# Attention mask of blocks 1 to 4: added by VectorE as scores leave PSUM, in place of two mask products on TensorE

## The chip, the core and the metric

The kernel runs on one core of one Trainium2 chip. The metric is the time of one execution on the device, in microseconds (us); the number that counts is the median of several runs.

## What is computed

The reference chains three stages. Only the first is touched by the change.

```python
# 1. windowed attention: batch 4, 8 heads, 576 positions, head size 64
scores = scale * np.matmul(q, k.transpose(0, 1, 3, 2))
rel = pos[:, None] - pos[None, :]
mask_plain = (rel >= 0) & (rel < 32)                          # heads 0 to 3
mask_dil = (rel >= 0) & (rel < 128) & (rel % 4 == 0)          # heads 4 to 7
scores = np.where(masks, scores, -1000000000.0)
scores = scores - np.max(scores, axis=-1, keepdims=True)
attn = np.exp(scores)
attn = attn / (np.sum(attn, axis=-1, keepdims=True) + 1e-09)
x = np.matmul(attn, v)                                        # to 2304 tokens x 512
# 2. gated layer: 512 -> 1536 -> 512
x = (sigmoid(x @ w_gate) * (x @ w_val)) @ w_out
# 3. soft mixture of 8 experts with 4 slots each (phi, w1, w2)
```

## The kernel before, in words

The 2304 tokens are cut into five blocks: blocks 0 to 3 are the first 512 positions of each batch entry, block 4 the last 64 positions of all four. A block has four **units**, one for each pair of heads, in the order `HP_ORDER = [0, 2, 1, 3]`. Block 0 is done first by itself. The 16 units of blocks 1 to 4 are called unit 0 to unit 15 here: units 0 to 3 are block 1, 12 to 15 block 4.

One unit goes through these steps:

- `scores`: TensorE fills two PSUM banks, one for each head (`s_ps`, pool `ps_a`). First one product a bank with the identity as weights and the bf16 mask as data (L148, 128x256), which writes 0 or a very negative number; then 32 small products of q and k (L162), which add to it.
- `weighted`: the products of attention weights and v for the unit two before (L222) go into the free columns of the same two banks.
- `softmax`: VectorE takes the row maximum of each bank (L176, two instructions), subtracts it (L178, two, which also bring the scores to SBUF, tile `sm` or, in block 4, the unit's own `qk` tile); ScalarE takes the exponential (L184); VectorE sums (L186), adds 1e-9 (L187), inverts (L188); GpSimd scales (L189).
- `turn_unit`: TensorE transposes the result (L195), ScalarE copies it out (L196).
- `finish_unit`: the weighted values leave PSUM through ScalarE (L237, L250) and VectorE (L238, L251).

These 16 units are spread, by the list `sab`, among the products of the gated layer of blocks 0 and 1 (`l1`, L470). There a **sum** is 12 products of 128x512 into one PSUM bank (pool `ps_l1`, two banks, used in turn); each of the 12 weight strips f has two sums, a = 0 (gate, taken out by ScalarE at L480) and a = 1 (value, taken out by VectorE at L456). The weights are split in two parts for exactness: ScalarE copies the high part (L433), VectorE or GpSimd subtracts it to give the low part (L434), into `whl`, a ring of two. The weights themselves arrive as 64-bit numbers and are converted first (`convert`): ScalarE L379, VectorE L380 and L381, GpSimd L382 (the sum of both halves into `fw`). Converted output weights are transposed by TensorE (L408, into `wt_ps`) and multiplied on (L414, L423).

Each engine runs its own instructions in order. TensorE's order around the units is the order in which the code is written (`at` keeps it there); the other engines' orders come from a scheduler that knows the priorities and what each instruction depends on. All loads and stores named here go through one queue, that of SP, in its order.

## Time and profile before

| | |
|---|---|
| median of 3 runs | 498.02 us (497.69 to 499.08) |
| the profiled execution | 496.94 us, of which the span of instructions is 495.2 us |
| TensorE (PE) busy | 468.6 us, 95% of the span |
| TensorE weight load (PEld) busy | 357.3 us, 72% |
| VectorE (DVE) busy | 311.0 us, 63% |
| ScalarE (ACT) busy | 213.1 us, 43% |
| GpSimd (POOL) busy | 156.8 us, 32% |
| mean granted TensorE clock | 0.992 of full speed |

Times in rows are counted from the first instruction. Matmuls are pipelined, so a row's duration of one product is longer than the step to the next; what a product costs TensorE is read from the starts of its neighbours. An engine's idle time costs nothing unless the engine is the one that sets the end.

### The profile page before, as it was taken

The page shows a single profiled execution, that of the slowest core. Times are in us where ns is not written, and L with a number is a line of the kernel's source. Part 1 is how long each engine was busy: PE and PEld are TensorE (multiplying, and loading weights), DVE is VectorE, ACT ScalarE, POOL GpSimd, SP SyncE. Part 2 cuts the span into 40 slices and gives each one's busy share as a digit, 9 for nine tenths or more (in the row PEclk, how much of TensorE's full clock was granted, in tenths as well). Part 3 has the DMA queues.
Part 4 walks back from the last instruction along what each step waited for, and adds up shares of the span by engine and source line. Part 5 has one row for each costly group of instructions (what it writes and reads, how often), then busy time and mean ns, then how long its engine had stood idle before and what let it go on. Part 6 is the DMA issues. An engine that isn't in the chain of part 4 may idle for free.

```text
span 495.2 us, 12830 instructions
## 1 busy us (share of the span) xinstructions
PE 468.6 (95%) x5488; PEld 357.3 (72%) x5488; DVE 311.0 (63%) x629; ACT 213.1 (43%) x414; POOL 156.8 (32%) x132
## 2 busy tenths in 40 slices
PE   6889999999899998999889999999999999999993
PEld 3558888887788876886557888888887889742552
DVE  3879898758666745436987656655547765541532
ACT  2455645435445534314744554554535343300223
POOL 0244536416445314235154323334212124110100
PEclk9899999999999999999999999999999999999998
DMA  8979978995896079120002201201499886579997
GB/s 301 421 276 361 351 234 306 310 344 195 322 368 253 2 253 394 63 86 1 1 1 86 85 25 61 86 5 80 142 372 422 345 326 259 190 296 367 428 402 239
DMA packets 23785, 112.14 MB, mean 226 GB/s; under 512 B 2352, under 2 KB 7216, under 8 KB 14640
## 3 DMA queue, kind: packets, MB, share of 16 engines
q1 hardware_dynamic: 23408, 111.06, 60.0%
q8 instruction: 43, 0.70, 0.6%
q10 hardware_dynamic: 320, 0.26, 0.2%
q14 instruction: 14, 0.11, 0.1%
HBM read 97.16 MB, written 14.16 MB: 225 GB/s over the span
## 4 chain that ended last, share of the span: by engine, by line
PE 80%; DVE 8%; DMA 4%; ACT 2%; issue 2%; POOL 1%; SPq 1%; DVEq 0%; ACTq 0%
PE l1ps L470 32%; PE pa L592 11%; PE pe L592 6%; PE tp L757 3%; PE s_ps L222 3%; PE h_ps L1045 3%; PE lt_ps L721 3%; PE pd L592 3%; PE s_ps L162 3%; PE so_ps L1104 3%; DMA wo<-fw 2%; PE sp L786 2%; PE tr L195 2%; DMA qk<-qkv 2%; DVE s L556 1%
## 5 line engine op out<-in xcount | busy, mean ns | idle before, releaser
L470 PE MATMUL l1ps<-x_hi,whl 128*128 128x512 f32 x384 | 129.4, 402 | 2.6 <-ACT x_hi L250 2.5
L470 PEld LDWEIGHTS l1ps<-x_hi,whl 128*128 128x128 f32 x384 | 71.7, 188 | 19.0 <-ACT x_hi L250 3.2
L470 PE MATMUL l1ps<-x_lo,whl 128*128 128x512 f32 x192 | 75.6, 394 | 0.0
L382 POOL TENSOR_TENSOR fw<-fw 128x512 int32<-128x512 int32 x36 | 49.0, 1370 | 61.7 <-DVE fw L381 24.7
L470 PEld LDWEIGHTS l1ps<-x_lo,whl 128*128 128x128 f32 x192 | 36.2, 188 | 6.6 <-DVE x_lo L251 0.2
L456 DVE SCALAR_TENSOR_TENSOR g<-g,l1ps 128x512 f32<-128x512 f32 (+1 forms) x36 | 21.4, 594 | 29.3 <-PE l1ps L470 29.0
L470 PE MATMUL l1ps<-x,whl 128*128 128x256 f32 x288 | 37.0, 285 | 0.0
L470 PEld LDWEIGHTS l1ps<-x,whl 128*128 128x128 f32 x288 | 35.4, 192 | 0.4 <-issue 0.2
L480 ACT ACTIVATE g<-l1ps 128x512 f32<-128x512 f32 (+1 forms) x36 | 18.9, 526 | 37.4 <-PE l1ps L470 37.4
L434 POOL TENSOR_TENSOR whl<-w,whl 128x512 fp32r<-128x512 f32 x12 | 15.9, 1326 | 51.2 <-ACT whl L433 39.7
L379 ACT ACTIVATE fw<-st 128x512 f32<-128x512 f32 x36 | 22.8, 675 | 12.4 <-DMA st<-wd 9.2
L757 PE MATMUL tp<-cst,g 128*128 128x128 f32 x216 | 28.0, 275 | 0.0
L757 PEld LDWEIGHTS tp<-cst,g 128*128 128x128 f32 x216 | 24.0, 140 | 5.0 <-issue 3.3
L762 ACT COPY gt<-tp 128x512 f32<-128x512 f32 x27 | 15.6, 584 | 25.0 <-PE tp L757 21.9
L176 DVE TENSOR_REDUCE mx<-s_ps 128x4 f32<-128x256 f32 x40 | 15.2, 413 | 14.3 <-PE s_ps L162 8.4
L380 DVE TENSOR_SCALAR fw<-fw 128x512 uint32<-128x512 uint32 x36 | 22.7, 640 | 1.9 <-ACT fw L379 1.0
L655 DVE TENSOR_TENSOR tm<-pe,tm 128x512 f32<-128x512 f32 x12 | 8.3, 691 | 24.1 <-PE pe L592 24.1
L434 DVE TENSOR_TENSOR whl<-fw,whl 128x512 fp32r<-128x512 f32 x24 | 20.9, 884 | 3.7 <-ACT whl L433 3.2
L381 DVE TENSOR_SCALAR fw<-st 128x512 int32<-128x512 uint32 x36 | 17.8, 528 | 7.7 <-DMA wst<-wg 3.7
L189 POOL TENSOR_TENSOR sm<-sm,su 128x512 f32<-128x512 f32 x12 | 13.6, 1130 | 28.3 <-DVE su L188 26.4
L434 POOL TENSOR_TENSOR whl<-wst,whl 128x512 fp32r<-128x512 f32 x12 | 15.9, 1326 | 19.0 <-ACT whl L433 11.7
L433 ACT CAST whl<-fw 128x512 fp32r<-128x512 f32 x24 | 14.6, 620 | 16.1 <-POOL fw L382 11.7
(455 smaller groups left out, 962.1 us busy)
## 6 DMA issues: line engine op xcount, KB each, us to landing
ew<-w SPq DMA_DIRECT2D x32, 1024.0 KB, 7.8
st<-wd SPq DMA_DIRECT2D x18, 1024.0 KB, 9.1
wst<-wg SPq DMA_DIRECT2D x12, 1024.0 KB, 7.7
v<-qkv SPq DMA_DIRECT2D x20, 512.0 KB, 6.1
wg<-fw SPq DMA_DIRECT2D x12, 512.0 KB, 7.8
w<-wg SPq DMA_DIRECT2D x6, 1024.0 KB, 7.5
qk<-qkv SPq DMA_DIRECT2D x10, 576.0 KB, 5.7
qk<-qkv SPq DMA_DIRECT2D x8, 528.0 KB, 5.5
```

The lines of the kernel that those rows point to most:

```text
L176: nc.vector.tensor_reduce(mx[:, 4 * r : 4 * r + 4], u["s_ps"][r], AX.X, ALU.max)
L379: nc.scalar.activation(top, st[:, c, 1].bitcast(F32), AF.Prelu, scale=2.0**-112, alpha=2.0**32)
L380: nc.vector.tensor_scalar(top.bitcast(U32), top.bitcast(U32), 3, None, ALU.logical_shift_left)
L381: nc.vector.tensor_scalar(low.bitcast(I32), st[:, c, 0], 2.0**-29, None, ALU.mult)
L382: nc.gpsimd.tensor_tensor(low.bitcast(I32), top.bitcast(I32), low.bitcast(I32), ALU.add)
L434: (nc.gpsimd if pool[h] else nc.vector).tensor_tensor(whl[:, 1, h], src[:, h], whl[:, 0, h].bitcast(F32), ALU.subtract)
L456: return nc.vector.scalar_tensor_tensor(g, g, 1.0, val, ALU.add, ALU.mult)
L470: nc.tensor.matmul(pt[:, 0:nt], lhsT=whl[:, w_, a, dc, :], rhs=x_[n][:, dc, :], start=first, stop=(dc == HP_ORDER[-1] and w_ == 1),)
L480: nc.scalar.activation(g, pt[:, 0:nt], AF.Tanh, scale=0.5)
L592: nc.tensor.matmul(pt, lhsT=w[:, w_, P * c : P * c + P], rhs=x_[:, c], start=first and c == 0 and w_ == 0 and x_ is hi, stop=c == 1 and w_ ...
L757: nc.tensor.transpose(tp[:, c], g_sb[self.n, 4 * q + c][:, P * j : P * j + P], ident)
L762: nc.scalar.copy(to, tp)
```

## The change

For units 0 to 15 the two mask products are left out, and the first product into each place of the scores starts the sum afresh (`start=True`). VectorE then does four instructions in place of four: two additions of mask and scores (each 128x256, PSUM and SBUF to SBUF), one maximum over the whole 128x512 tile in SBUF, and one subtraction of 128x512 from SBUF to SBUF. Block 0 (`head` is given) runs the old code.

```diff
-            for r in range(2):
+            for r in range(0 if u["added"] else 2):
                 at(
                     nc.tensor.matmul(
                         u["s_ps"][r].rearrange("p t c -> p (t c)"),
...
-                            start=False,
+                            start=u["added"],
...
-        for r in range(2):
-            nc.vector.tensor_reduce(mx[:, 4 * r : 4 * r + 4], u["s_ps"][r], AX.X, ALU.max)
-        for r in range(2):
-            nc.vector.tensor_tensor(
-                s[:, 4 * r : 4 * r + 4],
-                u["s_ps"][r],
-                mx[:, 4 * r : 4 * r + 4].unsqueeze(2).to_broadcast([P, 4, 64]),
-                ALU.subtract,
-            )
+        if u["added"]:
+            n, hp = u["id"]
+            m = mask[:, 2 if n == 4 else (1 if hp >= 2 else 0)].rearrange("p (t c) -> p t c", t=4)
+            for r in range(2):
+                nc.vector.tensor_tensor(s[:, 4 * r : 4 * r + 4], u["s_ps"][r], m, ALU.add)
+            nc.vector.tensor_reduce(mx, s, AX.X, ALU.max)
+            nc.vector.tensor_tensor(s, s, mx.unsqueeze(2).to_broadcast([P, 8, 64]), ALU.subtract)
+        else:
...
-        us = [{"id": j, "z": z} for z, j in enumerate(jobs)]
+        us = [{"id": j, "z": z, "added": not head} for z, j in enumerate(jobs)]
```

The scheduler orders the engines anew. Three places matter below. From line 192 on the changed kernel's lines are numbered 8 higher: its L442 is L434 of before, L464 is L456, L194 is L186, L196 is L188, L388 and L389 are L380 and L381, L416 is L408, L478 is L470.

VectorE around unit 2, before (the maximum is L176, the subtraction L178; `x_lo` belongs to unit 0, `fw` to the conversion of weights, `g` to a value sum):

```order
L176 TENSOR_REDUCE mx_936<-s_ps0_868 128x4
L380 TENSOR_SCALAR fw_845<-fw_845 128x512
L176 TENSOR_REDUCE mx_936<-s_ps1_869 128x4
L178 TENSOR_TENSOR sm4_172<-s_ps0_868,mx_936 128x256
L178 TENSOR_TENSOR sm4_172<-s_ps1_869,mx_936 128x256
L251 TENSOR_TENSOR x_lo_950<-s_ps0_868,x_hi_949 128x2x128
L456 SCALAR_TENSOR_TENSOR g_612<-g_612,l1ps_956 128x512
L186 TENSOR_REDUCE su_942<-sm4_172 128x8
```

The same place now (L179 adds the mask, L180 is the maximum, L181 the subtraction):

```order
L179 TENSOR_TENSOR sm4_172<-s_ps0_864,msk_75 128x256
L388 TENSOR_SCALAR fw_841<-fw_841 128x512
L179 TENSOR_TENSOR sm4_172<-s_ps1_865,msk_75 128x256
L259 TENSOR_TENSOR x_lo_944<-s_ps0_864,x_hi_943 128x2x128
L180 TENSOR_REDUCE mx_930<-sm4_172 128x8
L464 SCALAR_TENSOR_TENSOR g_612<-g_612,l1ps_950 128x512
L181 TENSOR_TENSOR sm4_172<-sm4_172,mx_930 128x512
L259 TENSOR_TENSOR x_lo_944<-s_ps1_865,x_hi_943 128x2x128
L442 TENSOR_TENSOR whl_1016<-fw_841,whl_1016 128x512
L194 TENSOR_REDUCE su_936<-sm4_172 128x8
```

The subtraction now stands behind the value sum's way out (L464), and the sum of the softmax (L194) behind half a weight split (L442).

VectorE at unit 14 (`su_2783` before, `su_2753` now) and the last conversion of output weights (`fw_2664` before, `fw_2636` now), before:

```order
L187 TENSOR_SCALAR su_2783<-su_2783 128x8
L188 RECIPROCAL su_2783<-su_2783 128x8
L381 TENSOR_SCALAR fw_2664<-st_2502 128x512 x2
L418 COPY pt_2836<-pt_ps_2831 128x256
L380 TENSOR_SCALAR fw_2664<-fw_2664 128x512 x2
```

Now:

```order
L195 TENSOR_SCALAR su_2753<-su_2753 128x8
L389 TENSOR_SCALAR fw_2636<-st_2476 128x512 x2
L196 RECIPROCAL su_2753<-su_2753 128x8
L426 COPY pt_2806<-pt_ps_2801 128x256
L388 TENSOR_SCALAR fw_2636<-fw_2636 128x512 x2
```

The reciprocal of unit 14 has moved from ahead of the conversion's first pair to behind it. GpSimd's order is the same in both kernels here: unit 14's scaling, then the two instructions of this conversion, then two weight splits.

TensorE at the same time, in block 1, strips f = 7 and 8 (`l1ps_2844` and `l1ps_2957` before), before:

```order
L408 MATMUL wt_ps_2838<-cst_76,fw_2664 128x128 x4
L470 MATMUL l1ps_2844<-x_hi_949,whl_2804 128x512 x2
L470 MATMUL l1ps_2844<-x_lo_950,whl_2804 128x512
L470 MATMUL l1ps_2844<-x_hi_949,whl_2804 128x512
L148 LDWEIGHTS msk_75
L148 MATMUL s_ps0_2858<-msk_75 128x256
L148 LDWEIGHTS msk_75
L148 MATMUL s_ps1_2859<-msk_75 128x256
L423 MATMUL wp_ps_2941<-cst_76,pt_2836 128x32 x2
L408 MATMUL wt_ps_2945<-cst_76,fw_2664 128x128 x4
L470 MATMUL l1ps_2957<-x_hi_949,whl_2951 128x512
```

Now:

```order
L478 MATMUL l1ps_2814<-x_hi_943,whl_2774 128x512
L416 MATMUL wt_ps_2808<-cst_76,fw_2636 128x128 x4
L478 MATMUL l1ps_2814<-x_hi_943,whl_2774 128x512
L478 MATMUL l1ps_2814<-x_lo_944,whl_2774 128x512
L478 MATMUL l1ps_2814<-x_hi_943,whl_2774 128x512
L431 MATMUL wp_ps_2909<-cst_76,pt_2806 128x32 x2
L478 MATMUL l1ps_2925<-x_hi_943,whl_2919 128x512
L478 MATMUL l1ps_2925<-x_lo_944,whl_2919 128x512
```

The mask products of unit 15 are gone, one product of the sum stands ahead of the first transposes, and the second four transposes have moved to a place behind unit 15's scores and weighted values. Everywhere earlier TensorE's order is that of before without the mask products. SP's order is unchanged.

## Rows read from the trace of the kernel before

**Rows 1.** Windows: length, then busy us (instructions) of PE, PEld, DVE, ACT, POOL.

```profile
34.00:50.00 16.00, 16.00 (x195) 12.51 (x194) 13.63 (x31) 8.27 (x16) 8.06 (x8) 1.00 0.83 303
50.00:70.00 20.00, 20.00 (x313) 16.16 (x314) 18.37 (x31) 10.94 (x20) 10.04 (x8) 1.00 0.84 295
104.00:175.00 71.00, 69.71 (x1322) 56.45 (x1321) 48.55 (x106) 34.21 (x66) 32.17 (x27) 1.00 0.64 236
```

**Rows 2.** TensorE's waits from 34 to 200 us: total, times, longest.

```profile
PE wt_ps L408 <- POOL fw L382: 1.4, 1, 1.4
PE s_ps L222 <- issue: 1.3, 1, 1.3
```

**Rows 3.** TensorE's timeline at unit 2's scores, then at unit 15's: start, duration.

```profile
51.56 0.39 PE L470 MATMUL l1ps<-x_hi,whl 128*128 128x512 f32 x1
51.79 0.39 PE L148 MATMUL s_ps<-msk 128*128 128x256 bf16 x2
52.11 0.86 PE L162 MATMUL s_ps<-qk 64*32 64x64 f32 x64
...
192.85 0.40 PE L470 MATMUL l1ps<-x_lo,whl 128*128 128x512 f32 x1
193.18 0.86 PE L162 MATMUL s_ps<-qk 64*32 64x64 f32 x64
```

**Rows 4.** VectorE's groups from 34 to 200 us: count, busy us, mean ns.

```profile
L434 DVE TENSOR_TENSOR whl<-fw,whl 128x512 fp32r<-128x512 f32 x20 | 17.6, 898 | 2.5 <-ACT whl L433 2.1
...
L176 DVE TENSOR_REDUCE mx<-s_ps 128x4 f32<-128x256 f32 x32 | 12.0, 413 | 7.2 <-PE s_ps L222 5.9 <-PE s_ps L162 1.3
...
L178 DVE TENSOR_TENSOR sm<-s_ps,mx 128x256 f32<-128x256 f32 x24 | 8.9, 410 | 0.0
L186 DVE TENSOR_REDUCE su<-sm 128x8 f32<-128x512 f32 x12 | 8.2, 683 | 3.7 <-ACT sm L184 3.4
```

**Rows 5.** VectorE's timeline from 35 to 65 us; the last row is GpSimd's.

```profile
35.94 0.76 DVE L176 TENSOR_REDUCE mx<-s_ps 128x4 f32<-128x256 f32 x2 [1.31 <-PE s_ps L162]
...
49.27 0.69 DVE L456 SCALAR_TENSOR_TENSOR g<-g,l1ps 128x512 f32<-128x512 f32 x1 [0.54 <-PE l1ps L470]
...
54.09 0.42 DVE L176 TENSOR_REDUCE mx<-s_ps 128x4 f32<-128x256 f32 x1 [0.46 <-PE s_ps L222]
...
62.05 2.39 DVE L434 TENSOR_TENSOR whl<-fw,whl 128x512 fp32r<-128x512 f32 x2
64.36 0.68 DVE L456 SCALAR_TENSOR_TENSOR g<-g,l1ps 128x512 f32<-128x512 f32 x1
64.96 1.28 DVE L434 TENSOR_TENSOR whl<-fw,whl 128x512 fp32r<-128x512 f32 x2
...
62.21 1.68 POOL L382 TENSOR_TENSOR fw<-fw 128x512 int32<-128x512 int32 x1 [0.36 <-DVE fw L381]
```

**Rows 6.** TensorE's timeline at the end of block 0's strip 5, sum a = 0.

```profile
65.28 0.62 PE L470 MATMUL l1ps<-x_hi,whl 128*128 128x512 f32 x2
```

**Rows 7.** The chain that ended last, 174 to 193 us: start, us, what.

```profile
174.85 0.45 PE tr L195 x4
...
177.06 8.92 DMA wo<-fw
...
186.08 0.76 DVE fw L381 x2
...
187.59 1.38 POOL fw L382
...
189.01 0.67 PE wt_ps L408 x4
...
190.95 1.29 POOL whl L434
...
192.28 0.97 PE l1ps L470 x3
```

**Rows 8.** GpSimd's timeline at unit 14's scaling.

```profile
184.69 1.04 POOL L189 TENSOR_TENSOR qk<-qk,su 128x512 f32<-128x512 f32 x1 [8.73 <-PE l1ps L470]
```

More of the change, by code (lines that the diff above doesn't have):

```diff
@@ L174, in softmax @@
         mx = sm.tile([P, 8], F32, tag="mx", name="mx")
-        for r in range(2):
-            nc.vector.tensor_reduce(mx[:, 4 * r : 4 * r + 4], u["s_ps"][r], AX.X, ALU.max)
-        for r in range(2):
-            nc.vector.tensor_tensor(
-                s[:, 4 * r : 4 * r + 4],
-                u["s_ps"][r],
-                mx[:, 4 * r : 4 * r + 4].unsqueeze(2).to_broadcast([P, 4, 64]),
-                ALU.subtract,
-            )
+        if u["added"]:
[6 more added lines that the diff above has]
+        else:
+            for r in range(2):
+                nc.vector.tensor_reduce(mx[:, 4 * r : 4 * r + 4], u["s_ps"][r], AX.X, ALU.max)
+            for r in range(2):
+                nc.vector.tensor_tensor(
+                    s[:, 4 * r : 4 * r + 4],
+                    u["s_ps"][r],
+                    mx[:, 4 * r : 4 * r + 4].unsqueeze(2).to_broadcast([P, 4, 64]),
+                    ALU.subtract,
+                )
         nc.scalar.activation(s, s, AF.Exp, scale=0.125)
```

## The prediction, made before the changed kernel was run

> **What bounds the kernel now.** I read the busy times stage by stage first, then TensorE's waits, then the timelines of TensorE and VectorE around single units, and last the chain that ended last. All 16 changed units lie between 35 and 194 us. There TensorE is busy nearly all the time: 16.00 of 16.00 us from 34 to 50, 20.00 of 20.00 from 50 to 70, 69.71 of 71.00 from 104 to 175 [rows 1]. Its waits in this stretch are few, and the two long ones are 1.4 us in front of the transposes of converted output weights and a gap of 1.3 us inside a run of small products for which no wait is shown [rows 2]. So TensorE sets the pace of the units, and an instruction less on it is time less, as long as what feeds it keeps up. VectorE is the engine next to the limit, but only early: 18.37 of 20.00 us busy from 50 to 70, against 48.55 of 71.00 later [rows 1]. The reader is to see that the change takes work from the engine that bounds and gives it to the one that is nearly full just there.
>
> After the units nothing is changed. What follows starts when the products of blocks 0 and 1 end, so I let it move with them.
>
> **What is removed: 32 mask products.** Their rows say more than they cost, since products overlap. With the pair, the step from the last product of a sum to the first score is 52.11 - 51.56 = 0.55 us; at unit 15, whose pair stands elsewhere, it is 193.18 - 192.85 = 0.33 us [rows 3]. A pair costs 0.22 us, 16 pairs 3.5 us. The first scores now start the sum afresh; they are the same instructions, and no row tells the two kinds of start apart by time: I take 0, and 0 is both bounds.
>
> Two of the 16 save nothing. From the transposes of unit 12 (174.85) the chain leaves TensorE: they free the tile that the next load in SP's queue waits for, behind that load a store goes out at 177.06 and takes 8.92 us, then VectorE, GpSimd and at 189.01 TensorE's L408, in front of which TensorE has waited; GpSimd's weight split releases it once more at 192.28 [rows 2, 7]. The code puts unit 13's pair ahead of unit 12's transposes, unit 14's between them and 189.01, and unit 15's ahead of 192.28. Without the last two TensorE only waits longer. 14 pairs are left: -3.1 us.
>
> **What is added on VectorE.** The additions take the place of the two maxima. The trace has no addition of a bf16 tile to PSUM; the nearest row is the subtraction L178 of the same size out of PSUM, 410 ns, against 413 ns for the maximum that goes [rows 4]. The other bound is the price of twice the elements, 683 ns; I take 410, since the element count is the same. Maximum and subtraction are now of 128x512 each. In a run, a second instruction of 128x512 adds 1.28 - 0.68 = 0.60 us and one of 128x256 adds 0.76 - 0.41 = 0.35 us [rows 4, 5]. So a unit costs VectorE 2 x 0.60 - 2 x 0.35 = 0.5 us more, and 8 us over 16 units.
>
> The subtraction also changes its kind: it has two operands in SBUF, where L178 had one in PSUM. The weight split L434 is such an instruction: two of them take 1.28 us at 64.96, but 2.39 us at 62.05, while GpSimd works from 62.21 to 63.89 [rows 5]; its mean is 898 ns [rows 4]. So a subtraction that meets GpSimd can cost 1.1 us more, one that doesn't nothing.
>
> The Trainium skill, in "SBUF — State Buffer", section "SBUF: two separate sides", says that VectorE with two SBUF operands and GpSimd take a shared port pair in turn, each for a whole instruction. By that rule the rows at 62 us agree (2.39 for 1.28), and each of the 16 subtractions is exposed for the first time; applied to every early one it gives the slower rival below.
>
> **Where VectorE's delay reaches TensorE.** From 104 us on VectorE idles 22 of 71 us [rows 1], and the unit's way from scores to transposes has microseconds to spare; I cost the added work there at nothing. Early it has a price. The tightest place is the way out of the value sum of block 0's strip 4: L456 starts at 64.36 and ends at 65.04 [rows 5], and the sum that takes its PSUM bank starts with the second product of the pair at 65.28, one step of 0.23 later, at 65.51 [rows 3, 6]. That is 0.47 us to spare, while three pairs saved by then make TensorE want the bank 0.66 us sooner. TensorE is thus held by VectorE's lateness plus 0.2 us.
>
> How late is VectorE there? Units 0, 1 and 2 give it 1.5 us more work, one meeting with GpSimd 1.1: 2.6 us. Its idle time from 34 to 70 us is 2.4 + 1.6 = 4.0 us [rows 1], of which 1.3 lies ahead of unit 0 [rows 5]. If all the remaining 2.7 us can be used, it is not late. If only the waits for TensorE can, 0.54 at 49.27 and 0.46 at 54.09 [rows 5], it is 1.6 us late: the other waits are for ScalarE's and GpSimd's part of the weight conversion, which moves with VectorE, and in the new order the exponential of unit 0 stands behind a sum's way out on ScalarE and unit 2's subtraction behind another on VectorE. Both ends are open; I take the middle, 0.9 us late, so TensorE loses 1.1 us (0.2 to 1.8, up to 5 in the rival below). Behind the late L456 stand the next two weight splits, whose sums start some microseconds after, so I charge nothing further.
>
> **What the new order moves at the end.** Unit 14's reciprocal now stands behind the first pair of the last conversion, which cannot start before the store has landed, at 186.08, and runs to 186.84 [rows 7]. GpSimd scales unit 14 after that reciprocal and, in its unchanged order, ahead of L382. Before, the scaling ran from 184.69 for 1.04 us and was long done when L382 started at 187.59 [rows 7, 8]. Now it starts near 187.2 and ends at 188.2 or, if it meets VectorE's next pair, 188.9: L382 starts 0.6 to 1.3 us later, and so do the transposes at 189.01 and the split at 190.95 that TensorE waits for. I take 1.0. If the reciprocal's result came before the store it would be 0. Four transposes that ran ahead of 192.28 now come after it (at most 0.67 us [rows 7]), and one product of 0.23 us ahead: 0.2 more, between 0 and 0.4.
>
> **The sum** is made against the profiled execution, 496.94 us: -3.1 + 1.1 + 1.2 = -0.8 us, 496.1 us. The median of the runs shown is 498.02, 1.1 us above that execution, so the same step gives 497.2 us. About 0.3%, 1.5 us, is what a measurement of this kernel can tell from no change.
>
> **The rivals.**
>
> *The saving comes through.* VectorE uses all its idle time (0.2 us lost), and the last conversion is not delayed: -3.1 + 0.2 = -2.9 us, 495.1 us. For it: TensorE's rows show no wait for VectorE at all now [rows 2], and the new order brings strip 5's first weight split (L442, in the rows of the order) ahead of the softmax sum. Against it: 0.47 us to spare at 65 us, and the reciprocal's new place.
>
> *The port decides: slower.* All three early subtractions meet GpSimd: VectorE is 1.6 + 2 x 1.1 = 3.8 us late at 65 us, or 4.8 if none of the idle time is used; TensorE loses 4.0 to 5.0 us, and the sum is -3.1 + 5.0 + 1.2 = +3.1 us at most, 501.1 us. It counts as slower from a lateness of 3.2 us (-3.1 + 3.4 + 1.2 = 1.5). The place is the same value sum of strip 4. For it: GpSimd is busy half of the time from 34 to 70 us [rows 1], so one meeting in two is likely. Against it: a meeting delays only what is behind it, and the weight splits that met GpSimd before need not meet it again.
>
> *The gap without a wait.* The 1.3 us inside the small products [rows 2] belongs to no engine. With 64 matmuls and weight loads fewer ahead of it, it may vanish (495.9) or a second one may come (498.5), and then the change itself tells little.
>
> **How the numbers follow.** My forecast 0.52, the saving 0.28, the port 0.14, the gap 0.06. The first spans -2.9 (0.2 and 0 lost) to +0.4 us (1.8 and 1.7): 495.1 to 498.4. The range for 8 in 10 goes into the rivals on both sides: 494.8 to 499.6. Faster by over 0.3% (below 496.5): the saving, a twentieth from the first: 0.33. Slower (above 499.5): the port and a little of the gap, 0.15. Within: 0.52.
>
> **What would show it.** The step from the last product of a sum to the first score is 0.33 us, not 0.55; no L148 behind block 0. VectorE has 32 additions near 410 ns, 16 maxima near 685 ns, and 16 subtractions of 680 ns or, where GpSimd runs, up to 1.8 us. TensorE waits 0.3 to 2 us in block 0's strips 4 and 5, with VectorE as releaser. GpSimd's scaling of unit 14 follows the store's landing, and TensorE's wait for L382's successor L390 grows from 1.4 to about 2.6 us. I am wrong if TensorE shows no such waits (the saving), or if its waits for VectorE add up to more than 3.4 us (the port), or if a wait appears that no row of before hints at.

## The result and the profile after

The changed kernel takes 503.93 us (median of 4 runs, 502.77 to 507.68); the kernel before, run beside it on the same chip, 498.55 us (4 runs, 497.69 to 499.74). The ratio is 1.0132, with a 95% interval of 1.0099 to 1.0164: slower by 5.4 us in the medians, where no change was forecast. Medians here and below are of all executions, while ratios and their intervals leave out those over 1.5% above the fastest of their kernel. The profiled execution has a span of 500.9 us (before 495.2) and a mean granted clock of 0.985 (before 0.992); the slowest of the four executions, 507.68 us, has the lowest mean clock, 0.973.

First the windows of the changed kernel; they answer to [rows 1], and the last three have no row there. The columns are start:end, length, busy us (instructions) of PE, PEld, DVE, ACT, POOL, the granted clock, the DMA share and GB/s.

```profile
34.00:50.00 16.00, 16.00 (x192) 12.64 (x192) 14.32 (x29) 8.10 (x15) 6.28 (x6) 1.00 0.84 309
50.00:70.00 20.00, 19.33 (x303) 15.45 (x304) 17.99 (x33) 10.34 (x19) 10.82 (x9) 1.00 0.81 295
104.00:175.00 71.00, 69.49 (x1318) 56.13 (x1316) 55.00 (x108) 35.28 (x68) 33.92 (x26) 1.00 0.65 238
...
190.00:194.00 4.00, 3.47 (x15) 2.70 (x16) 2.07 (x3) 2.66 (x5) 3.26 (x4) 0.76 1.03 418
194.00:198.00 4.00, 3.61 (x120) 2.71 (x120) 1.79 (x2) 0.00 (x0) 1.24 (x1) 0.81 0.86 316
198.00:202.00 4.00, 3.25 (x22) 2.82 (x22) 2.48 (x6) 1.02 (x3) 0.00 (x0) 0.62 0.56 232
```

Up to 175 us little is lost: VectorE does 6.45 us more from 104 to 175, and TensorE is as busy as before. Between 190 and 202 us the granted clock is below 1.00, which it never was there before. TensorE's waits from 34 to 200 us, answering to [rows 2] (total us, times, longest):

```profile
PE wt_ps L416 <- POOL fw L390: 3.2, 1, 3.2
PE s_ps L230 <- issue: 2.4, 3, 1.1
PE l1ps L478 <- DVE g L464: 1.1, 2, 0.7
PE l1ps L478 <- ACT x_hi L258: 0.8, 1, 0.8
PE s_ps L230 <- ACT pt_ring L204: 0.3, 1, 0.3
```

The wait in front of the transposes grew from 1.4 to 3.2 us, and in place of one gap of 1.3 us for which no wait is named ("issue") there are three, 2.4 us together. Where the time went is read from the start of the same product in both traces:

| first product of | before, us | after, us | later by |
|---|---|---|---|
| block 0, strip 0, a = 1 | 29.30 | 29.37 | 0.1 |
| block 0, strip 5, a = 0 | 62.79 | 62.13 | -0.7 |
| block 1, strip 0, a = 0 | 112.04 | 112.47 | 0.4 |
| block 1, strip 4, a = 1 | 155.31 | 154.39 | -0.9 |
| block 1, strip 7, a = 1 | 185.53 | 184.86 | -0.7 |
| block 1, strip 9, a = 0 | 201.38 | 206.72 | 5.3 |
| end of the span | 495.2 | 500.9 | 5.7 |

So the changed kernel is 0.7 us ahead at 185 us, and loses 6.0 us in the next 22 us. TensorE's timeline of the changed kernel there (start, duration; in brackets the idle time before and what ended it):

```profile
190.35 0.66 PE L416 MATMUL wt_ps<-cst,fw 128*128 128x128 f32 x4 [3.16 <-POOL fw L390]
191.08 0.40 PE L478 MATMUL l1ps<-x_lo,whl 128*128 128x512 f32 x1
...
192.26 0.80 PE L478 MATMUL l1ps<-x_hi,whl 128*128 128x512 f32 x1 [0.18 <-ACT whl L441]
192.85 0.63 PE L478 MATMUL l1ps<-x_lo,whl 128*128 128x512 f32 x1
193.28 1.56 PE L478 MATMUL l1ps<-x_hi,whl 128*128 128x512 f32 x3
...
195.84 0.86 PE L162 MATMUL s_ps<-qk 64*32 64x64 f32 x64
196.63 0.98 PE L230 MATMUL s_ps<-pt_ring,v 64*64 64x16 f32 x51
198.75 0.49 PE L230 MATMUL s_ps<-pt_ring,v 64*64 64x16 f32 x13 [1.14 <-issue]
199.17 1.11 PE L416 MATMUL wt_ps<-cst,fw 128*128 128x128 f32 x4
```

A product of 128x512 takes 0.63 us where it took 0.40: that is the granted clock at its lower level, 1.2 GHz for 2.4. The 8 products from 192.26 to 195.84 take 3.58 us, at a step of 0.23 they would take 1.84: 1.7 us lost. The transposes and five products from 199.17 to 202.22 lose about 1.5 us in the same way. The sum: 1.8 us of a longer wait, 3.2 us of a slower clock, 1.1 us for the gap of 198.75, less 0.2 us for a pair of mask products: 5.9 of the 6.0 us. (The wait of 0.18 us for ScalarE has one of 0.15 us for GpSimd in its place before.) The prediction has 1.0 of them.

The chain that ended last, through the wait (it answers to [rows 7, 8]):

```profile
175.98 10.42 DMA wo<-fw
...
186.50 0.76 DVE fw L389 x2
187.26 0.12 DVE su L196
...
187.61 1.28 POOL qk L197
188.90 1.41 POOL fw L390
...
190.35 0.67 PE wt_ps L416 x4
```

The store left 1.08 us earlier than before and landed 0.4 us later (10.42 us for 8.92); the DMA share was 1.00 from 186 to 190 us. Behind it come the conversion's pair, the reciprocal that now stands there, GpSimd's scaling (1.28 us) and only then the sum for the transposes, L390, at 188.90, 1.3 us later than before. This is the step that the prediction named.

### The profile page after: what moved, and what is told of

The parts are those of the page before. It is cut to its first block, busy times and chain, and to the rows that moved or that the text cites. A ratio compares the mean times of both kernels' runs of the same rounds, so it can differ in the third digit from the quotient of the medians.

```text
span 500.9 us, 12758 instructions
## 1 busy us (share of the span) xinstructions
PE 467.9 (93%) x5451; PEld 357.5 (71%) x5456; DVE 322.8 (64%) x629; ACT 213.9 (43%) x414; POOL 157.6 (31%) x132
## 4 chain that ended last, share of the span: by engine, by line
PE 61%; DVE 10%; DMA 7%; ACT 2%; issue 2%; POOL 2%; SPq 0%; DVEq 0%; POOLq 0%; ACTq 0%
PE l1ps L478 20%; PE pa L600 11%; PE pe L600 6%; PE tp L765 3%; PE lt_ps L729 3%; PE pd L600 3%; PE so_ps L1112 2%; DMA ew<-w 2%; PE s_ps L230 2%; DMA wo<-fw 2%; PE sp L794 2%; DMA st<-wd 2%; PE s_ps L162 1%; PE wt_ps L416 1%; PE h_ps L1053 1%
## 5 line engine op out<-in xcount | busy, mean ns | idle before, releaser
L478 PE MATMUL l1ps<-x_hi,whl 128*128 128x512 f32 x384 | 132.0, 408 | 3.8 <-ACT x_hi L258 2.5
L478 PEld LDWEIGHTS l1ps<-x_hi,whl 128*128 128x128 f32 x384 | 73.0, 191 | 21.3 <-ACT x_hi L258 3.2
L478 PE MATMUL l1ps<-x_lo,whl 128*128 128x512 f32 x192 | 76.7, 400 | 0.0
L390 POOL TENSOR_TENSOR fw<-fw 128x512 int32<-128x512 int32 x36 | 48.7, 1359 | 63.5 <-DVE fw L389 27.5
L478 PEld LDWEIGHTS l1ps<-x_lo,whl 128*128 128x128 f32 x192 | 36.8, 191 | 7.0 <-issue 0.4
L464 DVE SCALAR_TENSOR_TENSOR g<-g,l1ps 128x512 f32<-128x512 f32 (+1 forms) x36 | 21.3, 591 | 26.7 <-PE l1ps L478 26.3
L478 PE MATMUL l1ps<-x,whl 128*128 128x256 f32 x288 | 37.0, 285 | 0.0
L478 PEld LDWEIGHTS l1ps<-x,whl 128*128 128x128 f32 x288 | 35.4, 192 | 0.4 <-ACT whl L441 0.2
L442 POOL TENSOR_TENSOR whl<-w,whl 128x512 fp32r<-128x512 f32 x12 | 15.9, 1326 | 51.2 <-ACT whl L441 39.7
L442 DVE TENSOR_TENSOR whl<-fw,whl 128x512 fp32r<-128x512 f32 x24 | 21.4, 902 | 5.5 <-ACT whl L441 4.8
L442 POOL TENSOR_TENSOR whl<-wst,whl 128x512 fp32r<-128x512 f32 x12 | 15.8, 1321 | 28.1 <-ACT whl L441 20.4
L388 DVE TENSOR_SCALAR fw<-fw 128x512 uint32<-128x512 uint32 x36 | 22.1, 630 | 0.5 <-ACT fw L387 0.3
L389 DVE TENSOR_SCALAR fw<-st 128x512 int32<-128x512 uint32 x36 | 19.7, 576 | 4.1 <-DMA st<-wd 2.0
L162 PEld LDWEIGHTS s_ps<-qk 64*32 64x32 f32 x1280 | 14.3, 107 | 9.5 <-issue 7.6
L162 PE MATMUL s_ps<-qk 64*32 64x64 f32 x1280 | 17.7, 228 | 3.3 <-issue 2.0
```

Of the source, the lines that this page charges most:

```text
L162: nc.tensor.matmul(u["s_ps"][r][32 * i : 32 * i + 32, t, :], lhsT=q[64 * r : 64 * r + 64, 128 * t + 32 * i : 128 * t + 32 * i + 32], rhs=k ...
L388: nc.vector.tensor_scalar(top.bitcast(U32), top.bitcast(U32), 3, None, ALU.logical_shift_left)
L389: nc.vector.tensor_scalar(low.bitcast(I32), st[:, c, 0], 2.0**-29, None, ALU.mult)
L390: nc.gpsimd.tensor_tensor(low.bitcast(I32), top.bitcast(I32), low.bitcast(I32), ALU.add)
L442: (nc.gpsimd if pool[h] else nc.vector).tensor_tensor(whl[:, 1, h], src[:, h], whl[:, 0, h].bitcast(F32), ALU.subtract)
L464: return nc.vector.scalar_tensor_tensor(g, g, 1.0, val, ALU.add, ALU.mult)
```

## The experiments

Four theories. **A**: the reciprocal of unit 14, behind the pair that waits for the store, makes GpSimd late; TensorE waits, and its clock falls behind the wait. **B**: VectorE's added work, or its meetings with GpSimd, cost the time. **C**: the gap at 198 us is what lets the clock fall. **D**, formed after the first four runs: TensorE pauses where a piece of its own program lands late, and which instructions that hits depends on how many rows stand ahead of them. The change takes 64 rows (32 weight loads, 32 products) out of TensorE's list.

All were timed in five rounds beside the kernel before on the same chip. Medians in us, ratios to that kernel before; in brackets the 95% interval.

| label | median | ratio |
|---|---|---|
| recip_first | 502.02 | 1.0116 (1.0078 to 1.0153) |
| recip_late | 499.12 | 1.0031 (1.0015 to 1.0048) |
| block1_only | 499.22 | 1.0034 (1.0015 to 1.0054) |
| late_blocks | 503.05 | 1.0095 (1.0063 to 1.0127) |
| first_and_rows_back | 502.37 | 1.0065 (1.0034 to 1.0097) |
| before_rows_fewer | 504.18 | 1.0134 (1.0102 to 1.0166) |
| after_rows_back | 504.10 | 1.0134 (1.0104 to 1.0163) |
| wait_filled | 501.30 | 1.0075 (1.0045 to 1.0106) |
| before_plus_64 | 499.33 | 1.0023 (0.9988 to 1.0059) |
| before_plus_128 | 501.06 | 1.0045 (1.0018 to 1.0072) |
| first_minus_64 | 499.70 | 1.0026 (0.9998 to 1.0053) |
| first_plus_128 | 501.69 | 1.0065 (1.0037 to 1.0092) |
| before_rows_192 | 506.61 | 1.0175 (1.0146 to 1.0203) |
| first_rows_64 | 499.19 | 1.0025 (0.9992 to 1.0057) |
| first_rows_128 | 501.74 | 1.0077 (1.0049 to 1.0105) |
| first_rows_192 | 501.87 | 1.0082 (1.0053 to 1.0112) |
| first_rows_64_filled | 502.07 | 1.0071 (1.0045 to 1.0098) |
| before_filled | 498.68 | 1.0001 (0.9976 to 1.0026) |

**The reciprocal's place.** recip_first is the changed kernel with an edge of order (`behind(x, y)` keeps x behind y on their engine, and waits for nothing), so that VectorE's reciprocal of unit 14 stands ahead of the last conversion's L389; recip_late is the kernel before with the opposite edge. No other row moves in either.

```diff
-            nc.vector.tensor_scalar(low.bitcast(I32), st[:, c, 0], 2.0**-29, None, ALU.mult)
+            low_ = nc.vector.tensor_scalar(low.bitcast(I32), st[:, c, 0], 2.0**-29, None, ALU.mult)
+            pinned_at[i, h] = low_
...
-        nc.vector.reciprocal(su, su)
+        recip = nc.vector.reciprocal(su, su)
+        if u["z"] == 14:
+            for h in range(2):
+                behind(pinned_at[len(turn) - 1, h], recip)   # recip_late: behind(recip, pinned_at[...])
```

> The changed kernel with one edge more: unit 14's reciprocal stands ahead of the last conversion's first pair on VectorE, as before the change; every other row of every engine stands as in the changed kernel. Theory A (the reciprocal that waits for the store makes GpSimd late, TensorE waits 3.2 us for L390's result, and its granted clock falls behind that wait): the wait is back at about 1.4 us, the granted clock stays at 1.0 from 175 to 205 us, and the kernel takes 497 to 498 us, some 6 us less than the changed one and a ratio of 0.997 to 1.000 to the kernel before. Theory B (VectorE's added work or its meetings with GpSimd cost the time, whatever the order): 502 us or more. Theory C (the gap of 1.1 us at 198 us, for which no wait is shown, is what lets the clock fall): the wait's 1.8 us alone come back, 502 us, and the clock still falls.

> The kernel before, mask products and all, with the reciprocal of unit 14 moved behind the last conversion's first pair on VectorE; no other row moves. Theory A: TensorE's wait in front of L408's transposes grows from 1.4 to about 3 us, the granted clock falls behind it, and the kernel takes 4 to 6 us more than before, 502 to 504.5 us, without any added work on VectorE. Theory B: no change, 499 us at most. The prediction's own term for it: 1.0 us more.

The wait moves the way theory A says, to 1.67 us in recip_first (1.4 expected) and to 2.35 us in recip_late (3 expected), as in these two rows of their TensorE timelines.

```profile
189.56 0.66 PE L428 MATMUL wt_ps<-cst,fw 128*128 128x128 f32 x4 [1.67 <-POOL fw L402]
```

```profile
190.32 0.66 PE L420 MATMUL wt_ps<-cst,fw 128*128 128x128 f32 x4 [2.35 <-POOL fw L394]
```

The time doesn't. The reciprocal's place is worth 1.05 us in recip_late (499.12 against 498.07), which is the prediction's term and a quarter of the least that theory A asked for; and putting it back leaves recip_first 4 us slower than the kernel before. Theory A holds for the wait and falls as the whole cause of the loss. The clock fell behind recip_first's wait of 1.67 us and not behind recip_late's 2.35 us. The 502.02 us of recip_first is what theories B and C had named. Theory C falls by the place: in the changed kernel the first slow products start at 192.26, ahead of the gap. Whether the gap had a part in the second fall, at 199 us, is not shown.

**Which blocks.** block1_only and late_blocks (the latter with recip_first's edge) change one condition:

```diff
-        us = [{"id": j, "z": z, "added": not head} for z, j in enumerate(jobs)]
+        us = [{"id": j, "z": z, "added": not head and j[0] == 1} ...   # late_blocks: j[0] > 1
```

> The mask is added by VectorE for block 1 alone (units 0 to 3); blocks 2 to 4 keep their products, and the last conversion has the order of before. Theory A with the prediction's middle term: four pairs save 0.9 us, TensorE loses 1.1 to 1.5 us to VectorE between 60 and 100 us, so +0.2 to +0.6 us, a ratio of 1.000 to 1.002. Theory B: 2 us or more slower. If block 1's price was a matter of one place only and is made good later: -0.9 us.

> The mask is added by VectorE for blocks 2 to 4 alone (units 4 to 15), with unit 14's reciprocal ahead of the last conversion's first pair. Theory A: ten pairs of 0.22 us come through and nothing is lost, -2.2 us, a ratio of 0.995 to 0.997, with no wait of TensorE for VectorE and the granted clock at 1.0 to 200 us; the place of the gap without a wait can add or take 1.2 us. Theory B: no better than the kernel before.

block1_only is 1.15 us slower, more than theory A's 0.6 and less than theory B's 2. From block 0's second sum to block 1's first it loses 0.5 us net, where four pairs saved and the prediction's 1.1 us make 0.2; most of the rest lies at the wait, 1.9 us long, and behind it, where the granted clock fell (0.77 from 188 to 192 us). late_blocks, which has none of the early work, is among the slowest: 1.0095. Theory A's saving of 2.2 us failed there, and theory B's words, no better than before, came true. But its trace shows no wait of TensorE for VectorE from 34 to 206 us; TensorE waited 4.2 us for nothing that the profile names (2.4 us of it at 199 us), and 1.9 us in front of the transposes. That speaks against theory B and for a cause in the gaps and the wait.

**The number of rows, changed in the warm-up.** first_and_rows_back is recip_first with 64 rows put back ahead of the first load's landing, after_rows_back the changed kernel with the same, before_rows_fewer the kernel before with 64 rows fewer.

```diff
-WARM = 8
-SMALL = 70
+WARM = 5       # before_rows_fewer, first_minus_64: 11 and 35
+SMALL = 105    # before_plus_128, first_plus_128: 3 and 139
```

> The kernel of recip_first with 64 rows more in TensorE's list, 32 products of 32 columns with their weight loads, all in the warm-up ahead of the first load's landing: so each row from unit 15 on stands at the number that it had before the change. Theory D (the gap without a wait, 0.9 to 2.4 us at 198 us in every kernel with the mask added in blocks 2 to 4, is TensorE waiting for the next piece of its own program, and comes there because 64 rows fewer stand ahead): no gap at 198 us, the packets of instructions land near 187, 197.5 and 205 us as before the change, no second fall of the clock behind it, and about 499 us, 3 us less than recip_first. Theory A (the long wait for L390's result alone) and theory B (VectorE): no change, 502 us, and the gap stays.

> The kernel before with 64 rows fewer in TensorE's list, taken from the warm-up (the order of a few rows on VectorE in block 0 changes too): the rows behind the units stand at the numbers of the changed kernel, and no mask is added on VectorE. Theory D: a gap of 0.9 to 2.4 us near 198 us, in some executions with a fall of the clock behind it, 1 to 4 us more than before, a ratio of 1.002 to 1.008. Theories A and B: no change.

> The changed kernel with the 64 rows back in the warm-up; the reciprocal stays behind the conversion. Theory D with the reciprocal's term: the gap at 198 us goes, the wait of 3 us and the fall of the clock behind it stay, about 501 us, 3 us less than the changed kernel and 1 to 2 us more than first_and_rows_back. Theories A and B: no change from the changed kernel's 503.9.

before_rows_fewer shows that such a loss needs neither theory A nor theory B: with its mask products in place and no work moved to VectorE it is 1.34% slower, as much as the changed kernel. The largest part of its loss stands in one place, TensorE's timeline of before_rows_fewer:

```profile
137.73 0.41 PE L222 MATMUL s_ps<-pt_ring,v 64*64 64x32 f32 x8 [2.30 <-issue]
138.07 1.11 PE L408 MATMUL wt_ps<-cst,fw 128*128 128x128 f32 x4
138.84 0.77 PE L470 MATMUL l1ps<-x_hi,whl 128*128 128x512 f32 x1
```

a pause of 2.30 us inside a unit's small products, and behind it the slower clock (0.77 us for a product), which took 1.5 us. (The rest, in the profiled execution: 1.5 us at the start, 1.7 us behind another fall of the clock at 445 us.) Theory D expected this pause near 198 us, so the place was missed. In first_and_rows_back and after_rows_back the gap at 198 us is gone, as expected, but one came at 87.6 us in both (2.49 and 1.39 us), in the first with a fall of the clock behind it; neither gained the 3 us. after_rows_back waited 4.5 us in front of the transposes, with a fall behind it. The two differ in the reciprocal's place alone, and their ratios are 1.0065 (1.0034 to 1.0097) and 1.0134 (1.0104 to 1.0163): at this count of rows its place costs 0.7% by the ratios and 1.7 us in the medians, more than recip_late's 1.05 us, so theory A has a part in the loss.

> The kernel before with 64 rows more in TensorE's warm-up, nothing else (two rows of VectorE in block 0 swap). Theory D, as the runs so far have left it (TensorE pauses where a piece of its own program lands late inside a run of small products; which run that is depends on the number of rows ahead of it, and a pause of over 1 us can let the granted clock fall behind it): the time moves by up to 6 us either way, 494 to 504 us, with a gap without a wait at another place than 126.56 us. If the count of rows doesn't matter (theories A and B): 498 us, as before.

> The kernel before with 128 rows more in TensorE's warm-up. Theory D: another time than before_plus_64 and the kernel before, 494 to 504 us, the gap at another place again. Theories A and B: 498 us.

> recip_first (all 16 units' masks on VectorE, the reciprocal ahead of the conversion) with 64 rows fewer in the warm-up. Theory D: the time follows the place of the gap and not the work on VectorE; over the four counts of rows (0, +64, +128, -64) this kernel's times lie among those of the kernel before at its four, within 1 us on their means. Theory B (VectorE's added work): 502 us at every count, 3 to 4 us above the kernel before at the same one.

> recip_first with 128 rows more in the warm-up. Theory D: as for first_minus_64, a time between 494 and 504 us that goes with the place of the gap; with no gap of over 0.5 us from 100 to 205 us it is 496 to 498 us. Theory B: 502 us.

before_plus_64 has no gap over 0.3 us without a named wait from 60 to 206 us, where theory D had one at another place; before_plus_128 has one of 1.66 us at 146.85. With these, each kernel has four counts of rows. The kernel before: 498.07, 499.33, 501.06 and 504.18 us (0, +64, +128, -64), a mean of 500.7. recip_first: 502.02, 502.37, 501.69 and 499.70 us, a mean of 501.4. The kernel before is ahead by 3 to 4 us at two counts, the two are within 1 us at the third, and recip_first is ahead by 4.5 us at the fourth; the means differ by 0.8 us. That is theory D's expectation and not theory B's. What spoils the comparison is the warm-up: with more or fewer of its products the first sum began 0.6 to 3.8 us later than in the kernel before.

**The number of rows, changed inside block 0.** Here the rows are small products behind block 0's value steps (`small(n)` issues n products of 32 columns, each with its weight load), and every other row of every engine keeps its place.

```diff
             if head:
                 keep_warm(WP)
+                small(12)      # 4, 8 or 12: 64, 128 or 192 rows
```

> The kernel before with 192 rows more in TensorE's list (96 products of 32 columns with their weight loads, 12 behind each value step of block 0); every other row of every engine keeps its place. The start costs 1 us at most. Theory D (the count of rows sets where TensorE's pause falls): a pause at another place than 126.56 us, and 499.5 to 504 us, as before_rows_fewer had it, whose rows stand at the same place within a piece of 256. Theory B (VectorE): 498 to 499 us.

> recip_first with 64 rows more, in the same manner (4 small products behind each value step). Theory D: the pause at 198 us goes and one comes elsewhere, at 87 us by the runs with the rows in the warm-up, 500 to 503 us. Theory B: 502 us, pause or no pause.

> recip_first with 128 rows more (8 small products behind each step). Theory D: no pause of over 0.9 us from 60 to 205 us, the end 0.5 us or more ahead of the kernel before once the start's cost is taken off, 496.5 to 499 us. Theory B: 502 us.

> recip_first with 192 rows more (12 small products behind each step). Theory D: as first_rows_128, no pause of over 0.9 us from 60 to 205 us, 496.5 to 499 us, against before_rows_192's 499.5 to 504 at the same count. Theory B: 502 us.

The start costs more than expected: 4 to 7 us at 128 and 192 rows, where 1 us at most was named. The added products themselves are not what costs: TensorE's timeline of before_rows_192 has three pauses there, and 12 products take 0.25 us.

```profile
11.56 0.38 PE L110 MATMUL idle<-pm 128*128 128x512 bf16 x1 [2.90 <-issue]
11.87 0.25 PE L115 MATMUL idle<-pm 128*32 128x32 bf16 x12
...
17.48 0.20 PE L115 MATMUL idle<-pm 128*32 128x32 bf16 x5 [0.82 <-issue]
...
23.60 0.85 PE L165 MATMUL s_ps<-qk 64*32 64x64 f32 x36 [2.98 <-issue]
```

The kernel before has two such pauses at its start, 0.59 and 0.71 us. To leave the start out, I also read the time from the first product of block 0's second sum to the end of the span, in the profiled executions:

| kernel | that product at, us | to the end, us |
|---|---|---|
| before | 29.30 | 465.9 |
| after | 29.37 | 471.5 |
| before_rows_fewer | 30.82 | 471.7 |
| before_rows_192 | 33.44 | 471.1 |
| first_rows_128 | 33.90 | 468.3 |
| first_rows_192 | 36.17 | 464.9 |
| first_rows_64 | 30.13 | 464.7 |

At the same count of 192 rows the kernel with the mask on VectorE is 4.7 us faster than the one without (501.87 against 506.61); at the original count it is 4 us slower. The timeline of before_rows_192 has a pause at nearly the same instructions as before_rows_fewer, whose rows stand at the same place within a piece of 256:

```profile
136.70 1.02 PE L225 MATMUL s_ps<-pt_ring,v 64*64 64x32 f32 x56
139.88 0.44 PE L225 MATMUL s_ps<-pt_ring,v 64*64 64x32 f32 x8 [2.16 <-issue]
...
141.02 0.78 PE L474 MATMUL l1ps<-x_hi,whl 128*128 128x512 f32 x1
141.59 0.63 PE L474 MATMUL l1ps<-x_lo,whl 128*128 128x512 f32 x1
```

and its windows show the clock behind it:

```profile
126.00:138.00 12.00, 11.72 (x287) 9.26 (x285) 8.13 (x17) 4.85 (x10) 6.84 (x6) 1.00 0.99 373
...
140.00:142.00 2.00, 2.00 (x14) 1.76 (x15) 1.63 (x5) 0.60 (x2) 2.00 (x2) 0.50 0.60 141
142.00:146.00 4.00, 4.00 (x11) 3.11 (x10) 0.98 (x3) 0.79 (x2) 0.07 (x1) 0.50 0.99 335
```

Theory D's figures were missed: before_rows_192 came out above its 499.5 to 504 us, first_rows_64 (499.19) below its 500 to 503 and without a pause at 87 us, first_rows_128 and first_rows_192 above their 496.5 to 499. The start ate the gain of the last two, and in first_rows_128 the clock also fell behind a wait of 2.27 us and again at 444 us. What holds is that the count of rows matters: first_rows_64 differs from recip_first in 64 rows alone, and the ratios are 1.0025 (0.9992 to 1.0057) and 1.0116 (1.0078 to 1.0153). (Their medians lie 1.9 and 4.0 us above the kernel before that ran beside them.) The work on VectorE is the same in both, so it is not what makes the difference. Without the start, first_rows_64 and first_rows_192 are 1.0 to 1.2 us ahead of the kernel before: what the mask on VectorE is worth where no long pause and no fall of the clock meet it. This is from one execution each.

**What the pause waits for.** The traces also hold the packets of the queue that carries instructions. Its row in the DMA view of before_rows_192 from 137.4 to 138.5 us, and of the changed kernel from 196.2 to 197.35 us:

```profile
q8 instruction: 1, 0.02, 5.3%
```

```profile
q8 instruction: 1, 0.02, 5.6%
```

One packet of 16 KB lies in each, and none between it and the pause's end (139.88 and 198.75 us). In the 20 traces of this case there are 23 pauses of over 0.6 us from 60 to 206 us that end 1.2 to 1.6 us behind the end of such a packet, 19 of them inside a run of a unit's small products; all the long pauses without a named wait are among them. The data queue fills the DMA engines there (share 0.99 from 126 to 138 us above).

A count settles more. Number TensorE's rows, weight loads and products together, from 0 in the order of their starts. All 23 pauses end at a row whose number is 191 to 194 above a multiple of 256, and so do the 8 shorter ones there, of 0.3 to 0.6 us without a named wait: 4034 = 15 x 256 + 194 for the kernel before at 126.56 us, 6335 = 24 x 256 + 191 for the changed kernel at 198.75. The three pauses at the start of before_rows_192 end at rows 449, 705 and 961, each 193 above such a multiple. And in the 20 whole traces, with 840 packets in all, row 256 n + 196 never started sooner than 1.0 us behind the end of the n-th packet. So each packet holds about 256 rows of TensorE's own program, and the pauses stand where the next piece has not come yet. No row of the profile names this wait; the count leaves little room for another reading. It also says what 64 rows do: they choose which instructions stand at these places.

In the Trainium skill, "Runtime: NRT & Kernel Launch", section "Instruction fetch mechanics", an engine's program arrives in blocks of 16 KiB, that is 256 instructions, and crossing from one to the next is called mostly hidden. The size agrees (43 packets, 0.70 MB, for 10,973 rows of TensorE in the changed kernel), and so does "mostly": of some 350 crossings from 60 to 206 us in the 20 traces 23 show, but as pauses of 0.7 to 2.5 us each.

**The wait filled.** Four products of 128x512 go into the bank that the transposes then overwrite, ahead of them.

```diff
             wt_ps = ps_a.tile([P, ND, P], F32, tag="a", name="wt_ps")
+            for y in range(4 if f == 10 and c == 0 else 0):
+                nc.tensor.matmul(wt_ps.rearrange("p k x -> p (k x)"), lhsT=msk[:, M_ID:M_COLS], rhs=msk[:, 0:512], ...)
```

> first_and_rows_back with four products of 128x512 on TensorE (0.9 us, into the bank that the transposes then overwrite) inside the wait in front of L390's transposes; the rows in the warm-up are fewer by as many. If what TensorE did in the wait decides whether the granted clock falls behind it: the clock at 1.0 from 190 to 200 us in nearly every execution, 1 to 1.7 us less than first_and_rows_back, near 497.5 us. If the clock falls for another reason: no change or 0.3 us more.

> first_rows_64 with four products of 128x512 on TensorE (0.9 us, into the bank that the transposes overwrite) in the wait ahead of L390's transposes; some products behind the wait change places. If the clock's fall behind the wait makes the spread: most executions at 495.5 to 498.5 us, a median of 497, 2 us below first_rows_64's, and hardly one above 501. If the spread comes from elsewhere (the start, the pauses): no change, 499 us.

> The kernel before with the same four products in the same wait. Its wait was 1.4 us and mostly without a fall of the clock behind it: 0 to 0.7 us less than before, a ratio of 0.998 to 1.000. If filling the wait only makes TensorE later: 0.5 us more.

In all three profiles the idle rest of the wait is under 0.9 us and the clock stays at 1.00 behind it; in the 17 profiles with the wait unfilled it fell within some microseconds of it in 8. But the time is not bought: wait_filled is no faster than first_and_rows_back (1.0075 against 1.0065), before_filled is the same as before, and first_rows_64_filled is 2.9 us slower than first_rows_64. In that trace a pause of 1.02 us stands at 86.6 us, VectorE makes TensorE wait 0.5 us at 204.7 us, where products had changed places, and the clock falls at 441 us. The spread between executions of first_rows_64 (496.35 to 505.83 us) is therefore not explained by this wait alone, and stays open. No version beat the kernel before beyond its interval.

## Why the prediction was wrong

The forecast was 497.2 us with no measurable change; measured were 503.93. The step that failed is the sum, -3.1 + 1.1 + 1.2. Behind the last conversion it charges a longer wait with its length alone: 1.0 us for the reciprocal, and of two pairs less it says that "TensorE only waits longer". And it prices all products at the step of 0.23 us, which is that of the full clock. The granted clock behind such a wait is no term of it: it was put at nothing, without a reason. The gap without a wait was kept out of the sum as well. In the profiled execution the stretch from 185 to 207 us lost 6.0 us in their place: 3.2 us to the lower clock, 1.8 us to the wait, 1.1 us to the gap, less 0.2 us for a pair of mask products. The sentence "What follows starts when the products of blocks 0 and 1 end, so I let it move with them" held: 5.3 us late at 207 us, 5.7 at the end.

The sum also counts a removed product as time and not as two rows of the program. The kernel before owes its 498 us in part to where its pauses lie: one of 1.3 us [rows 2], no fall of the clock behind it. Taking 64 rows out without moving any mask costs 1.3% (before_rows_fewer), and 64 rows more in block 0 bring recip_first from 1.0116 to 1.0025 (first_rows_64). What stays open is why the clock falls behind one wait or pause and not behind another of the same length; so the split of the 6.0 us holds for the one profiled execution.

- **The rival that named it was mis-sized.** "The gap without a wait" saw that 64 rows fewer could move or double the gap, at 1.3 us either way and a chance of 0.06. The gaps measured run from nothing to 2.5 us. Behind the four longest, 2.2 to 2.5 us, the clock fell each time (in before_rows_fewer this took 1.5 us more); behind one of 2.05 us it did not.
- **14 pairs, -3.1 us:** right where it can be seen. The step from a sum to the scores is 51.47 - 51.15 = 0.32 us (below), 0.33 forecast; after three pairs TensorE was 0.67 us ahead. But only 0.7 us of the saving was left at 185 us, where the store's landing ended it: the store left 1.08 us earlier and landed 0.4 us later. So what was saved ahead of that wait only made the wait longer. The prediction applied this to two pairs; it held for what was left of all.
- **VectorE's prices:** additions 415 ns for 410, maxima 676 for about 685, subtractions 681 or 781 for 680, in the groups of the changed kernel below. Of the 16 subtractions 13 took 0.68 to 0.69 us, three 0.82, 1.06 and 1.32 us: 1.2 us more for all 16. These three began while GpSimd's sum L390 ran, and each ended 0.54 to 0.55 us behind that sum's end; a fourth, which began 0.16 us ahead of GpSimd's, took 0.68 us. By the rule of the Trainium skill in "SBUF — State Buffer", section "SBUF: two separate sides", whichever of the two starts first holds the shared ports for its whole instruction, and the other waits. These four rows agree. Of the three early subtractions one met GpSimd, as charged, but at 0.14 us and not 1.1.

```profile
L181 DVE TENSOR_TENSOR sm<-sm,mx 128x512 f32<-128x512 f32 x12 | 9.4, 781 | 0.1
L179 DVE TENSOR_TENSOR sm<-s_ps,msk 128x256 f32<-128x256 f32 x24 | 9.1, 415 | 3.4 <-PE s_ps L230 2.3 <-PE s_ps L162 1.1
...
L180 DVE TENSOR_REDUCE mx<-sm 128x8 f32<-128x512 f32 x12 | 8.1, 676 | 0.1
...
L181 DVE TENSOR_TENSOR qk<-qk,mx 128x512 f32<-128x512 f32 x3 | 2.0, 681 | 0.0
```

- **Block 1's +1.1 us:** right in kind and place. TensorE's timeline of the changed kernel, which answers to [rows 3, 6], and VectorE's way out of strip 4's value sum:

```profile
51.15 0.39 PE L478 MATMUL l1ps<-x_hi,whl 128*128 128x512 f32 x1
51.47 0.86 PE L162 MATMUL s_ps<-qk 64*32 64x64 f32 x64
...
64.62 0.39 PE L478 MATMUL l1ps<-x_hi,whl 128*128 128x512 f32 x1
65.68 0.50 PE L478 MATMUL l1ps<-x_hi,whl 128*128 128x512 f32 x1 [0.67 <-DVE g L464]
...
79.87 0.50 PE L478 MATMUL l1ps<-x_hi,whl 128*128 128x512 f32 x1 [0.43 <-DVE g L464]
```

```profile
64.95 0.67 DVE L464 SCALAR_TENSOR_TENSOR g<-g,l1ps 128x512 f32<-128x512 f32 x1
```

  VectorE is 0.6 us late there (64.95 for 64.36 [rows 5]; 0.9 forecast), and TensorE starts its next product at 65.68 and not a step of 0.23 us behind 64.62: 0.8 us lost. Two more such holds, 0.6 us at 79.87 and 0.3 us near 94, were not charged. So from block 0's second sum to block 1's first the net is +0.4 us, where the seven pairs saved by then and 1.1 us lost would have made -0.4. TensorE's waits for VectorE add up to 1.1 us in all, far from the 3.4 of the rival in which the port decides: it is refuted although the time came out on its side.
- **The reciprocal, +1.0 us:** right. GpSimd's scaling stands in the chain as forecast, and recip_late measures 1.05 us. The wait became 3.2 us and not 2.6 us, since TensorE also came earlier. What the term lacks is the clock behind the wait: 1.7 us in the profiled execution, not in each.

## What to carry to other kernels

When an edit adds or removes many short instructions, time both versions at several counts of padding rows before believing either: here the kernel before moved by 1.3% with 64 rows fewer, several times what the edit itself was worth. To see whether a gap without a named wait belongs to the program's pieces, count the rows ahead of it, as above. Read a gap without a named wait as a price that moves with every edit ahead of it, and look at the granted clock behind each long wait. And follow a saving to the next wait that DMA ends: here most of what was left of it was waited out there.

## What the runs showed of the hardware

- TensorE paused 0.7 to 2.5 us without a named wait 23 times, 19 of them inside runs of small products, each time 191 to 194 rows above a multiple of 256 and 1.2 to 1.6 us behind the landing of a packet of the instruction queue. The n-th packet landed when TensorE stood at most 290 rows short of row 256 n + 192, where its pauses end (840 packets).
- 192 rows of tiny products, 96 weight loads and 96 products of 32 columns in block 0, cost 4 us of start in before_rows_192, though 70 of these products take 0.7 us in the warm-up: three pauses at the program's pieces, 6.7 us together, stand there, against 1.3 us in the kernel before.
- The wait in front of the transposes let the clock fall in one kernel's profiled execution and not in another's, and its length does not tell which: waits of 1.7, 1.9, 1.9, 2.2, 2.3, 2.5, 3.2 and 4.5 us had a fall behind them, waits of 1.4, 1.6, 1.6, 1.7, 1.7, 1.7, 1.7, 2.0 and 2.4 us had none.
